# Two banks for the buckets' sums, one-hots for two buckets at once, and four smaller edits in a graph kernel

## The chip, the cores and the metric

The kernel runs on one core of one Trainium2 chip. A core has five engines with instruction queues of their own: TensorE (PE for matmuls, PEld for the loads of its stationary operand), VectorE (DVE), ScalarE (ACT), GpSimd (POOL) and SyncE (SP, which issues most of the plain DMAs). They meet by semaphores. The metric is the device time of one execution in microseconds, the median of several runs.

## The reference

A message-passing step of an equivariant graph network, all in float32: N = 10,000 nodes with 64 channels of 4 components, E = 640,000 edges with random ends `src` and `dst`.

```
R   = silu(edge_feat @ w_rad)                   # (E, 64), edge_feat is (E, 4)
xs  = x[src]                                    # (E, 64, 4)
tp  = einsum('eci,ef,ifo->eco', xs, Y, cg)      # (E, 64, 4), Y is (E, 4), cg is (4, 4, 4)
msg = R[:, :, None] * tp
agg = segment_sum(msg, dst, N)                  # (N, 64, 4)
out = einsum('ncm,cd->ndm', agg, w_mix)         # (N, 64, 4)
```

## The kernel before, in words

The nodes are cut into 313 **buckets** of at most 32 nodes, and the buckets into 20 **groups** of 15 or 16. The edges, 5000 tiles of 128, are cut into three parts by `SPLIT` (1488, 1776 and 1736 tiles). Each part is sorted by destination in two passes, and then its messages are computed bucket by bucket. Five tiles of 128 slots hold a bucket's edges of the first part, six those of the second and of the third.

**Sorting.** A pass takes chunks of T tiles (`pass1` sorts edges into groups with T = 16 in the first part and T = 24 in the others, 74 and 73 chunks; `pass2` sorts a group's edges into buckets with T = 24). `digits` and `tables` count the edges of each (tile, digit) and turn the counts into a table of starting places for several chunks at once: a count by matmul (`cnt`), a scan on VectorE (`sums`), small matmuls (`prep`, `fo`), and arithmetic on [chunks, digits]. The table that the chunks use, `sb`, holds places times the number of digits B plus the digit, as two bf16 rows. `route` then moves the chunks, in half-chunks called pieces: `places` spreads the table over the partitions by matmuls into PSUM (`pp`), `placed` copies it out on ScalarE (`pc`), `slots` finds each edge's row and slot on VectorE, `spread` builds the products `X` of slot masks and payloads on VectorE (in the first part, the last `self.spare` tiles of each piece on GpSimd), `onehots` builds a one-hot matrix per tile (the last `self.act` tiles on ScalarE), `move` runs one float32 matmul per tile with the one-hots as stationary operand, `evict` copies the result out on ScalarE, and `store` scatters its rows to DRAM with an indirect DMA of GpSimd. An edge's payload is 9 words: a key of source and destination, Y and edge_feat. `chunk` in `pass1` puts it together in `Wt`.

**Messages.** `messages` goes over units; a unit is one bucket in one part, so there are 3 × 313 = 939. For unit k: `index` (per group) takes source rows and local node numbers from the payload; `gather` issues one indirect DMA per tile on GpSimd for the rows of x, into one of seven buffers `xg`; `rests`, `spell`, `turn`, `turned`, `radial` and `silu` compute R with bf16 pieces of edge_feat through TensorE and ScalarE; `spots` compares local node numbers with 0 to 31 into `eq` and multiplies by Y, which gives `S`; `products` multiplies the gathered rows by R in place; `sums` runs two float32 matmuls per tile and adds up `G`, 128 × 256 numbers, in PSUM; `evict` takes `G` out: a copy on ScalarE in the first part (`Gp`), an addition to the earlier parts' sums `old` on VectorE in the second (`Gp`) and third (`Gs`). `fetch` loads `old` from DRAM on SP's queue, and the sums of the first two parts are stored by SP too. In the third part `full` and `mix` end four buckets with 8 float32 matmuls and write the output.

**Order of the work.** The sort of the first part runs alone in the first 750 us or so, with a compiler's order on all engines but SP. After that the order on TensorE, VectorE and ScalarE is the one in which the code emits the instructions. `groups` interleaves three streams: `messages`, `pass2` one group ahead, and `pass1` of the next part. `messages` emits a step in four quarters, given by `quarters` (line 1048): each entry is a function and how many units ahead of k it works. After each quarter the two sorts emit some of theirs. Unit k's sums come in the first quarter of step k, its eviction in the third, behind the products of unit k+1.

**PSUM.** Eight banks: one for constants and masks (`dv`, of which columns 128 to 511 are `vmsk`, the place of `eq` and of the slot masks), one `misc` for `cnt`, `prep`, `fo` and the mix, one `pos` for `pp`, two `route`, two `pre` and one `G`. `self.held` is a lock on `misc` in the order of emission, and `self.pos` one on `pos`: a stream that finds them taken yields "held", and `groups` lets the holder go on.

```
            if k % 2 and 0 <= k + 7 < NP:
                while self.pos:
                    yield "held"
                self.pos = ps.key
                places((k + 7) // 2)
            if k % 2 == 0 and 0 <= k + 6 < NP:
                placed((k + 6) // 2)
                self.pos = None
```

## Time and profile before

| | us |
|---|---|
| median of 3 runs | 9961.38 |
| lowest, highest | 9958.73, 9973.47 |
| the profiled execution | 9973.83 |
| its span, first to last instruction | 9971.9 |
| mean granted TensorE clock | 0.824 |

| engine | busy us | share of the span |
|---|---|---|
| PE | 7409.9 | 74% |
| PEld | 6726.3 | 67% |
| DVE | 6683.2 | 67% |
| ACT | 4025.3 | 40% |
| POOL | 5821.9 | 58% |

The profile names an instruction by its line in the kernel, its engine, and the tiles that it writes and reads (`G<-S,xg` is written to G and reads S and xg). "Idle before" is the time in which the engine stood just before an instruction, and the name behind `<-` is what ended most of it. "issue" means that nothing the profile shows was waited for, and "remote" that a semaphore ended the wait whose setter the profile could not name. A float32 matmul is recorded as two matmul instructions and two loads. The granted clock is the share of its full rate that TensorE was given.

### The profile page before, as it was taken

Reading aid. Unit: us, or ns where it says so; the run is one execution under the profiler, and the core shown is the slowest. Engines: PE = TensorE matmul, PEld = TensorE weight load, DVE = VectorE, ACT = ScalarE, POOL = GpSimd, SP = SyncE. Lnnn points to the kernel's source line nnn. Section 1 sums busy time; section 2 is a strip of 40 time slices with the busy share of each in tenths; the row PEclk is TensorE's granted clock in tenths of the full one; section 3 lists DMA queues with packets and bytes.
Section 4 is the critical chain, followed back from the end, with each engine's and each line's share of the span. In section 5 each row is a group of like instructions: output and inputs, shape, how many; then the busy total and the mean of one; then the engine's idle time right before and its main releaser. Section 6 shows DMA issues by size and latency. Waiting matters only on the chain. (4 is left out here: it accounts for less than half of the span.)

```text
span 9971.9 us, 143192 instructions
## 1 busy us (share of the span) xinstructions
PE 7409.9 (74%) x50081; PEld 6726.3 (67%) x50081; DVE 6683.2 (67%) x11771; ACT 4025.3 (40%) x11208; POOL 5821.9 (58%) x6222
## 2 busy tenths in 40 slices
PE   6886777877787678877777777676677776777764
PEld 5765776777776677776667677665666666676664
DVE  7885677777776677777777777565555555565543
ACT  4663454555554444444334344232232332332220
POOL 3635555555556556655555656666666666666663
PEclk8987888888887888888888888877888887888886
DMA  5113333333333334443433444444333333333331
GB/s 233 47 37 101 105 101 100 106 103 103 104 106 106 108 108 119 121 118 112 119 107 109 119 117 114 126 120 119 110 108 112 113 109 109 113 111 110 111 110 55
DMA packets 680544, 1086.82 MB, mean 109 GB/s; under 512 B 255649, under 2 KB 485103, under 8 KB 673552
## 3 DMA queue, kind: packets, MB, share of 16 engines
q0 software_dynamic: 282224, 774.67, 26.9%
q1 hardware_dynamic: 396448, 295.26, 10.1%
q8 instruction: 397, 6.50, 0.3%
q10 hardware_dynamic: 1152, 7.74, 0.2%
q14 instruction: 323, 2.65, 0.1%
HBM read 855.30 MB, written 222.79 MB: 108 GB/s over the span
## 5 line engine op out<-in xcount | busy, mean ns | idle before, releaser
L894 POOL DMA_INDIRECT xg<-in_x_dram,sidx x5321 | 5086.7, 956 | 3282.7 <-issue 1401.3
L982 PE MATMUL G<-S,xg 128*128 128x128 f32 x21284 | 3263.0, 316 | 951.4 <-issue 405.5
L982 PEld LDWEIGHTS G<-S,xg 128*128 128x128 f32 x21284 | 3049.4, 228 | 1054.0 <-issue 477.5
L612 PE MATMUL pr<-X,oh 128*128 128x81 f32 (+14 forms) x20530 | 3034.9, 306 | 731.5 <-issue 377.9
L612 PEld LDWEIGHTS pr<-X,oh 128*128 128x128 f32 x20530 | 2849.3, 215 | 859.5 <-issue 476.0
L971 DVE TENSOR_TENSOR xg<-xg,pre 128x1536 f32<-128x1536 f32 (+1 forms) x939 | 1557.6, 1659 | 413.7 <-ACT pre L953 294.3
L601 ACT ACTIVATE oh<-i,row 128x128 f32<-128x128 f32 x5322 | 1654.3, 391 | 94.9 <-PE pr L612 83.9
L585 DVE TENSOR_TENSOR X<-dv,Wt 128x2052 f32<-128x2052 f32 (+11 forms) x814 | 1336.9, 1642 | 414.8 <-remote 176.7
L953 ACT ACTIVATE pre<-pre 128x384 f32<-128x384 f32 (+1 forms) x939 | 430.8, 459 | 2491.6 <-remote 938.3
L964 DVE TENSOR_TENSOR S<-dv,pay 128x768 f32<-128x768 f32 (+1 forms) x939 | 857.6, 913 | 220.6 <-remote 111.8
L602 ACT ACTIVATE oh<-oh,ones 128x768 f32<-128x768 f32 (+1 forms) x1000 | 862.6, 863 | 31.4
L1011 DVE TENSOR_TENSOR Gs<-old,G 128x256 f32<-128x256 f32 x313 | 131.7, 421 | 1053.8 <-remote 603.6
L597 DVE TENSOR_TENSOR oh<-dv,row 128x768 f32<-128x768 f32 (+3 forms) x960 | 796.9, 834 | 6.8 <-PE pr L612 6.7
L941 ACT ACTIVATE sT<-pre 108x256 bf16<-108x256 bf16 x939 | 354.0, 377 | 703.8 <-remote 389.0
L552 ACT ACTIVATE pc<-pp 128x480 f32<-128x480 f32 (+8 forms) x500 | 236.1, 472 | 799.2 <-remote 260.5
L937 PE MATMUL pre<-idb,E 128*108 128x128 bf16 x1878 | 295.1, 241 | 313.0 <-DVE xg L971 124.8
L937 PEld LDWEIGHTS <-E 128*108 128x108 bf16 x1878 | 226.3, 143 | 381.8 <-issue 185.9
L631 POOL DMA_INDIRECT grp<-rt,idx x240 | 274.6, 1144 | 300.4 <-DVE dv L579 60.0
L949 PE MATMUL pre<-wr,sT 108*128 108x192 bf16 x1878 | 331.9, 260 | 136.0 <-ACT sT L941 76.0
L631 POOL DMA_INDIRECT bkt<-rt,idx x260 | 260.3, 1001 | 280.2 <-ACT rt L624 88.1
L1011 DVE TENSOR_TENSOR Gp<-old,G 128x256 f32<-128x256 f32 x313 | 130.8, 418 | 435.0 <-remote 257.5
L1030 PE MATMUL po<-wf,Gs 128*128 128x256 f32 (+1 forms) x1280 | 323.4, 408 | 33.0 <-DVE kov L524 17.6
(277 smaller groups left out, 5062.3 us busy)
## 6 DMA issues: line engine op xcount, KB each, us to landing
xg<-in_x_dram,sidx POOLq DMA_INDIRECT x5321
sums<-Gp SPq DMA_DIRECT2D x626, 128.0 KB
old<-sums SPq DMA_DIRECT2D x626, 128.0 KB
bkt<-z SPq DMA_DIRECT2D x26, 1024.0 KB
grp<-z SPq DMA_DIRECT2D x16, 1024.0 KB
pay<-bkt SPq DMA_DIRECT2D x208, 54.0 KB
out_dram<-ot SPq DMA_DIRECT2D x69, 128.0 KB
grp<-z ACTq DMA_DIRECT2D x7, 1024.0 KB
```

Source lines behind the costliest of these rows:

```text
L585: eng.tensor_tensor(X[:, b:e], msk[:, b:e].unsqueeze(3).to_broadcast([P, e - b, w, W]), CH[c][1][:, a + b:a + e, :].unsqueeze(2).to_broadc ...
L597: nc.vector.tensor_tensor(oh[:, :v, :], self.v128.unsqueeze(1).to_broadcast([P, v, P]), row[:, a:a + v].unsqueeze(2).to_broadcast([P, v, P ...
L601: nc.scalar.activation(oh[:, u], self.i128[:, :oh.shape[2]], AF.Square, bias=row[:, a + u:a + u + 1], scale=-1.0)
L602: nc.scalar.activation(oh[:, v:m], oh[:, v:m], AF.Relu, bias=self.ones[:, 0:1], scale=-2.0)
L612: nc.tensor.matmul(PR[c][:, ps.lo[t] * W:ps.hi[t] * W], oh[:, u, :], Xs[u], start=(t == 0), stop=(t == sizes[c] - 1), skip_group_check=True)
L631: nc.gpsimd.indirect_dma_start(out=ps.dst, out_offset=bass.IndirectOffsetOnAxis(ap=idx[:Q, i:i + 1], axis=0), in_=RT.pop(c), in_offset=None)
L894: nc.gpsimd.indirect_dma_start(out=xg[:, t, :], out_offset=None, in_=self.x, in_offset=bass.IndirectOffsetOnAxis(ap=si[:, u:u + 1], axis=0))
L937: nc.tensor.transpose(to[:108, h * P:(h + 1) * P], E[:, o + h * 108:o + h * 108 + 108], self.idb)
L953: nc.scalar.activation(RT[k], RT[k], AF.Silu)
L964: nc.vector.tensor_tensor(S[:, :ut], self.eq[:, :ut].unsqueeze(3).to_broadcast([P, ut, NB, 4]), pb[:, :, 1:5].unsqueeze(2).to_broadcast([P ...
L971: nc.vector.tensor_tensor(V, V, R.unsqueeze(3).to_broadcast([P, ut, 64, 4]), op=OP.mult)
L982: nc.tensor.matmul(G[:, h].rearrange("p n f -> p (n f)"), V[:, t, 32 * h:32 * h + 32, :].rearrange("p c i -> p (c i)"), S[:, t].rearrange( ...
```

## The change

It has six parts.

1. `G` gets two PSUM banks instead of one. The bank comes from `pos`: `pp` now lives in `misc`. In the messages the eviction comes one unit later (`evict` at -1), `full` at -2, `fetch` at 2 in the last quarter instead of 4 in the first, and `old` has three buffers instead of four.
2. In `route`, `places` and `placed` are emitted together at the end of each odd step, when `misc` is free, and `self.pos` is gone.
3. `spots` works on every second unit and makes `eq` and `S` for two buckets at once; `S` and `eq` are twice as long, and `dlc` is laid out so that two buckets' numbers lie side by side.
4. In `tables`, the counts are multiplied by B as ScalarE copies them from PSUM, and the lower bounds `low` carry the factor and the digit from the start, so `sums` holds places as the table wants them. `at` and its scaling go; the bf16 copy is made on ScalarE; the row of totals is divided by B again on VectorE. The two copies `ovr` and, in `pass1`, the copy of the key into `Wt` move from VectorE to ScalarE.
5. First-pass chunks of the second and third part have 22 tiles instead of 24 (81 and 79 chunks).
6. One-hot matrices have Q columns instead of 128 (Q is 120 in the first pass, 128 in the second), and `self.spare` in the first part is 4 instead of 3.

```diff
-        early, late = some(16), some(T)
+        early, late = some(16), some(22)
...
-        self.eq = self.vmsk[:, :UT * NB].rearrange("p (t n) -> p t n", n=NB)
+        self.eq = self.vmsk[:, :2 * UT * NB].rearrange("p (t n) -> p t n", n=NB)
...
-        nc.scalar.activation(cols[:, :, 1:m + 1], cnt[:H, :m * B].rearrange("p (t b) -> p b t", b=B), AF.Copy)
+        nc.scalar.activation(cols[:, :, 1:m + 1], cnt[:H, :m * B].rearrange("p (t b) -> p b t", b=B), AF.Copy,
+                             scale=float(B))
...
-        n = w("n", B, 32)
-        nc.vector.tensor_copy(n[:N], sums[:N, :, m])
+        n, ni = w("n", B, 32), w("ni", B, 32, d=I32)
+        nc.vector.tensor_scalar(ni[:N], sums[:N, :, m], 1.0 / B, 0.5 / B - 0.5, op0=OP.mult, op1=OP.add)
+        nc.vector.tensor_copy(n[:N], ni[:N])
+        sb = wk.tile([H, ps.T * B], BF, name="sb", tag="sb" + ps.key, bufs=3)
+        tb = sb[:, :m * B].rearrange("p (t b) -> p b t", b=B)
+        nc.scalar.activation(tb, sums[:, :, :m], AF.Copy)
...
-        nc.vector.scalar_tensor_tensor(tb(at), sums[:, :, :m], float(B),
-                                       self.v128[:H, :B].unsqueeze(2).to_broadcast([H, B, m]), op0=OP.mult, op1=OP.add)
-        nc.vector.tensor_copy(sb[:, :m * B], at[:, :m * B])
-        nc.vector.tensor_tensor(sb[32:, :m * B], at[32:, :m * B], sb[32:, :m * B], op=OP.subtract)
+        nc.vector.tensor_tensor(tb[32:], sums[32:, :, :m], tb[32:], op=OP.subtract)
...
-        nc.vector.tensor_copy(two[:, 0], rep(over[:N, :B]))
-        nc.vector.tensor_copy(two[:, 1], rep(inc[:N]))
+        nc.scalar.activation(two[:, 0], rep(over[:N, :B]), AF.Copy)
+        nc.scalar.activation(two[:, 1], rep(inc[:N]), AF.Copy)
...
-            pp = self.ps.tile([P, 512], F, name="pp", tag="pos", bufs=1)[:, :m * B]
+            pp = self.ps.tile([P, 512], F, name="pp", tag="misc", bufs=1)[:, :m * B]
...
-            oh = self.ph.tile([P, ps.H, P], F, name="oh", bufs=3)
+            oh = self.ph.tile([P, ps.H, P], F, name="oh", bufs=3)[:, :, :Q]
...
-            if k % 2 and 0 <= k + 7 < NP:
-
-                while self.pos:
-                    yield "held"
-                self.pos = ps.key
-                places((k + 7) // 2)
-            if k % 2 == 0 and 0 <= k + 6 < NP:
-                placed((k + 6) // 2)
-                self.pos = None
...
+            if k % 2 and 0 <= k + 7 < NP:
+                while self.held:
+                    yield "held"
+                places((k + 7) // 2)
+                placed((k + 7) // 2)
...
-            nc.vector.tensor_copy(Wt[:, :m, 0].bitcast(I32), SB[b][:, o:o + m])
+            nc.scalar.activation(Wt[:, :m, 0], SB[b][:, o:o + m].bitcast(F), AF.Copy)
...
+            if j % 2:
+                return
+            ut = tiles(k)[1]
+            b = min(2, self.nb(g[1]) - j)
+            n = b * ut
+            pb = self.pay[g][:, j:j + b].rearrange("p b (t w) -> p (b t) w", w=W)
+            dl = IDX[g][1][:, j * ut:(j + b) * ut]
+            nc.vector.tensor_tensor(self.eq[:, :n], self.i32.unsqueeze(1).to_broadcast([P, n, NB]),
+                                    dl.unsqueeze(2).to_broadcast([P, n, NB]), op=OP.is_equal)
+            S = ph.tile([P, 2 * UT, NB, 4], F, name="S")
+            nc.vector.tensor_tensor(S[:, :n], self.eq[:, :n].unsqueeze(3).to_broadcast([P, n, NB, 4]),
+                                    pb[:, :, 1:5].unsqueeze(2).to_broadcast([P, n, NB, 4]), op=OP.mult)
+            for i in range(b):
+                SS[k + i] = S[:, i * ut:(i + 1) * ut]
...
-                GP[g, j] = self.ps.tile([P, 2, NB, 4], F, name="G", tag="G", bufs=1)
+                GP[g, j] = self.ps.tile([P, 2, NB, 4], F, name="G", tag="G", bufs=2)
...
-                OLD[g, j] = ph.tile([P, 2, 4, NB], F, name="old", bufs=4)
+                OLD[g, j] = ph.tile([P, 2, 4, NB], F, name="old", bufs=3)
...
-        quarters = (((index, LI), (gather, LG), (fetch, 4), (turn, 2), (sums, 0), (silu, 1)), ((rests, 4), (turned, 2), (spots, 1)),
-                    ((products, 1), (evict, 0)), ((spell, 3), (radial, 2), (full, -1)))
+        quarters = (((index, LI), (gather, LG), (turn, 2), (sums, 0), (silu, 1)), ((rests, 4), (turned, 2), (spots, 1)),
+                    ((products, 1), (evict, -1)), ((spell, 3), (radial, 2), (full, -2), (fetch, 2)))
...
-            self.rt_bufs, self.ls, self.act, self.spare = 20, 10, 3, 3
+            self.rt_bufs, self.ls, self.act, self.spare = 20, 10, 3, 4
```

41 lines of the change are left out of this document (17 added, 24 removed).

## The prediction

> **What bounds the kernel now.** I read the page's busy shares first, then the busy time by stage. The second part of the run (from 830 us) has three stages, one for each share of the edges; they end where the `Gp` evictions move from ScalarE to VectorE and become `Gs`. Columns: us, busy time and instructions of PE, PEld, DVE, ACT and POOL, granted clock, DMA share, GB/s.
>
> ```profile
> span 9971.9 us, 143192 instructions
> ...
> PE 7409.9 (74%) x50081; PEld 6726.3 (67%) x50081; DVE 6683.2 (67%) x11771; ACT 4025.3 (40%) x11208; POOL 5821.9 (58%) x6222
> ...
> 0.00:830.00 830.00, 628.93 (x4242) 541.67 (x4242) 650.52 (x1566) 486.39 (x1433) 354.11 (x525) 0.85 0.30 102
> 830.00:3680.00 2850.00, 2202.32 (x15297) 2013.05 (x15297) 2040.32 (x3598) 1388.88 (x3923) 1665.11 (x1727) 0.84 0.37 105
> 3680.00:6917.00 3237.00, 2440.97 (x16619) 2223.71 (x16617) 2303.13 (x3691) 1279.70 (x3458) 1938.93 (x2021) 0.83 0.41 117
> 6917.00:9854.00 2937.00, 2107.18 (x13836) 1928.45 (x13837) 1651.55 (x2746) 865.16 (x2375) 1846.79 (x1934) 0.81 0.38 110
> ```
>
> No engine is full in any stage. With 313 buckets a stage, a bucket takes 9.1, 10.3 and 9.4 us, and PE works 7.0, 7.8 and 6.7 us of it. So waits set the pace. The list of waits (total us, times, longest) says which:
>
> ```profile
> POOL xg L894 <- issue: 1401.3, 4501, 10.2
> ACT pre L953 <- remote: 938.3, 149, 20.0
> ...
> POOL xg L894 <- PE G L982: 782.3, 220, 14.1
> DVE Gs L1011 <- remote: 603.6, 114, 10.9
> ...
> PE G L982 <- DVE Gs L1011: 279.7, 67, 11.0
> ACT pc L552 <- remote: 260.5, 34, 14.2
> ...
> ACT pc L552 <- PE pp L546: 201.7, 54, 10.7
> ...
> PE G L982 <- DVE Gp L1011: 171.6, 42, 9.2
> ...
> PE pre L937 <- DVE xg L971: 124.8, 86, 6.1
> ...
> PE pr L612 <- DVE oh L597: 104.9, 51, 8.5
> ...
> PE G L982 <- ACT Gp L1013: 81.0, 29, 8.7
> ```
>
> The largest wait of PE for anyone is for the eviction of the one bank `G`: 279.7 + 171.6 + 81.0 = 532 us in 138 waits. The evictions themselves wait for PE, often under the name "remote". POOL too waits for PE's sums to free a gather buffer, so it too could go faster than it is let. A stretch of the timeline (start, length, engine) shows the knot:
>
> ```profile
> 9563.54 2.94 PE L982 MATMUL G<-S,xg 128*128 128x128 f32 x24 [1.27 <-DVE Gs L1011]
> ...
> 9566.49 0.28 PE L937 MATMUL pre<-idb,E 128*108 128x128 bf16 x2
> ...
> 9573.92 0.95 POOL L894 DMA_INDIRECT xg<-in_x_dram,sidx  x1 [0.31 <-issue]
> 9577.32 0.42 DVE L1011 TENSOR_TENSOR Gs<-old,G 128x256 f32<-128x256 f32 x1 [10.91 <-remote]
> 9577.42 0.47 ACT L953 ACTIVATE pre<-pre 128x384 f32<-128x384 f32 x1 [12.52 <-remote]
> 9577.56 0.95 POOL L894 DMA_INDIRECT xg<-in_x_dram,sidx  x1 [2.69 <-remote]
> ...
> 9577.80 4.42 PE L982 MATMUL G<-S,xg 128*128 128x128 f32 x19 [11.04 <-DVE Gs L1011]
> ```
>
> PE's sums are over by 9566.5 on record, yet the eviction, the silu and POOL's next gather all start within 0.24 us at 9577.3, 2.4 us after POOL's last gather ended (9573.92 + 0.95). I read that as PE's completions reaching the others late while POOL streams gathers. Whatever the reason, PE and DVE both stand for 11 us here, because the next sums need the bank, the bank needs the eviction, and the eviction needs the late completion.
>
> **The change part by part.** The sum starts from the profiled execution, 9973.8 us (span 9971.9 and 1.9 around it); that is 12.4 above the median of the runs, 9961.4.
>
> (A) *Second bank for `G`, eviction one bucket later.* In such a stall PE may now run the next bucket's sums: their products were finished before it (the eviction follows them on DVE). Then it stops at the radial matmuls, whose input ACT copies only after a completion of PE. So a stall gives back at most one bundle of sums, 2.94 us by the row above: 138 × 2.94 = 406 us; many of the 138 are shorter (mean 3.9 us). I take −300, between 0 (the same late completion holds the silu, and nothing comes sooner) and −532. DVE and, in the first stage, ACT no longer hold the work queued behind the eviction (spread and one-hots of the sort), which is why I stay near the upper half. `fetch` moves three buckets ahead of its use instead of four, 3 × 9.4 = 28 us before the eviction, and passes the sort's loads on SP's queue; 128 KB would take 1.2 us at the 110 GB/s of the third stage's row, an estimate, so 0, and if it were late the eviction would hold DVE again. `full` one later: one step at the very end, 0.
>
> (B) *Less on DVE.* The forms that carry it (busy, mean ns):
>
> ```profile
> L964 DVE TENSOR_TENSOR S<-dv,pay 128x768 f32<-128x768 f32 x626 | 599.5, 958 | 26.5 <-remote 5.0
> ...
> L964 DVE TENSOR_TENSOR S<-dv,pay 128x640 f32<-128x640 f32 x313 | 258.2, 825 | 194.1 <-remote 106.8 <-PE G L982 29.2 <-PE pre L937 23.6
> ...
> L961 DVE TENSOR_TENSOR dv<-dv,dlc 128x192 f32<-128x192 f32 x626 | 226.0, 361 | 6.8
> ...
> L734 DVE COPY Wt<-si 128x24 int32<-128x24 int32 (+2 forms) x240 | 50.6, 214 | 51.3 <-POOL X L585 51.3
> ...
> L484 DVE SCALAR_TENSOR_TENSOR at<-sums,dv 64x336 f32<-64x336 f32 (+7 forms) x92 | 76.5, 832 | 0.0
> ...
> L486 DVE CAST sb<-at 64x336 bf16<-64x336 f32 (+7 forms) x92 | 33.4, 363 | 3.0
> ...
> L500 DVE COPY ovr<-inc 4x128 f32<-4x128 f32 (+4 forms) x92 | 22.3, 242 | 0.1
> ...
> L585 DVE TENSOR_TENSOR X<-dv,Wt 128x2052 f32<-128x2052 f32 x131 | 300.7, 2296 | 48.5 <-PE pr L612 28.1 <-remote 8.9 <-issue 4.6
> ...
> L585 DVE TENSOR_TENSOR X<-msk,Wt 128x540 f32<-128x540 f32 (+1 forms) x186 | 184.4, 994 | 25.9 <-ACT Wt L733 25.9
> ```
>
> 128 more elements cost `S` 133 ns, so 1.04 ns each, and 160 ns are fixed; `dv`, by the same slope, has about 160 fixed too. One pair saves one of each, 0.33 us; 13 groups of 16 buckets and 7 of 15 make 153 pairs a stage, 459 in all: −150. `at` goes (−76), its cast moves to ACT (−33); a conversion of a row's last column is added (+15). Two `ovr` copies like the one shown and the `Wt` copy move to ACT (−42, −51). Chunks of 22 tiles are at most 18 slots wide where 24 tiles reached 19: from the slot bounds in the code the products shrink by 31,400 elements (−33), and one-hots of 120 columns give about −20; 13 more chunks and 2 more tables bring +40. In all about −350 of 6683. Little of it is on the path: apart from the eviction, PE waits for DVE for 125 + 105 us, 3% of the time. I take −40, between 0 and −350. The pair's longer `S` (958 → 1757 ns) delays the products every second bucket by 1.1 us; the second bank covers that.
>
> (C) *ACT, and places and placed together.* ACT gets the copies, about +150 us of 4025; its idle time before the silu, 938 us under "remote" alone, hides them. The new wait is the other one: `placed` now stands directly behind its matmuls, where it stood half a step later, so ACT must wait for PE's 0.8 us and a completion that may be late; queued behind it on ACT are silu, turned and one-hots, and PE waits for those. It also shares `misc` with tables and mix. Before, 88 such waits cost ACT 462 us. The stages have 160 + 260 = 420 chunks. From 0 (ACT would have stood anyway) to 420 × 1.4 = 590 us; I take +60, near the end at which ACT has slack.
>
> (D) *13 more chunks* (81 + 79 for 74 + 73), each with a store on POOL (row below) and about 2 us on ACT and 0.8 on PE: 17 us on POOL, 26 on ACT; +20 (0 to 40).
>
> (E) *First stage (to 830 us, DVE 78% busy).* One of five product tiles goes to POOL: a fifth of 184.4 us, −37 on DVE, with its share of (B); POOL, at 43%, takes about a third more of its products and stays below. −25, between 0 and −60.
>
> (F) *One-hots of 120 columns as PE's stationary operand, narrower moving one.* No first-pass row shows 120 columns. The nearest is the final mix, 128 against 96:
>
> ```profile
> L631 POOL DMA_INDIRECT grp<-rt,idx x240 | 274.6, 1144 | 300.4 <-DVE dv L579 60.0 <-ACT rt L622 57.4 <-DMA grp<-z 49.2
> ...
> L612 PEld LDWEIGHTS pr<-X,oh 128*128 128x128 f32 x20530 | 2849.3, 215 | 859.5 <-issue 476.0 <-ACT rt L622 130.0 <-DVE oh L597 113.9
> ...
> L1030 PEld LDWEIGHTS po<-wf,Gs 128*128 128x128 f32 x1168 | 227.8, 200 | 57.2 <-issue 15.4 <-DVE kov L524 8.0 <-DVE ko L522 2.4
> ...
> L1030 PEld LDWEIGHTS po<-wf,Gs 128*96 128x96 f32 x112 | 24.8, 229 | 22.8 <-DVE kov L524 11.9 <-issue 0.7
> ```
>
> By these rows fewer columns load no faster (229 against 200 ns): 10,000 first-pass loads × 29 ns = +290 at worst; the narrower chunks' moving operand saves some 40. A gain for columns in proportion would be 200 × 8/128 = 12 ns, −125. I take −30. The Trainium skill (TensorE: Matmul & The Clock Gate, LDWEIGHTS) says that a load takes its columns ÷ 1.2 in ns; by that, eight columns are 6.7 ns, an estimate of −67 us, which would make the sum 9562 in place of 9599; the row of 96 columns does not agree, though the clock may differ between the two rows.
>
> (G) *Clock.* Two stretches, before and after the stall shown above, granted clock after the busy times:
>
> ```profile
> 9554.00:9567.00 13.00, 10.44 (x94) 9.91 (x91) 6.63 (x8) 3.47 (x10) 8.95 (x10) 1.00 0.43 127
> 9578.00:9583.00 5.00, 5.00 (x24) 5.00 (x25) 3.10 (x4) 0.18 (x1) 3.78 (x5) 0.50 0.38 108
> ```
>
> PE idles and comes back at half rate (24 sums in 2.94 us before, 19 in 4.42 after). With fewer stalls I put the stages' clock 0.011 up: 7409.9 × 0.011/0.83 = 98 us less PE work, two thirds on the path, −60 (0 to −200, at 0.85). The Trainium skill's same page (A second HAM failure mode: psum-queue depth-cycling) speaks against the change: a kernel that went round its PSUM banks paused so often between groups of matmuls that its clock swung between half and full. By that rule (G) is 0 and the sum 9659; the trace has the swing already with one bank, in the two rows above.
>
> Sum: −300 −40 +60 +20 −25 −30 −60 = −375; 9973.8 − 375 = 9599, and 12 less against the median: **9590 us**, −3.7%.
>
> **Rivals.**
> 1. *The wait moves to the silu.* In the stall shown, ACT's silu stood 12.5 us for the same moment. If every stall is like that, (A) keeps 60 and (G) nothing: 9973.8 − 60 − 15 = 9899, 9890 against the median. For: ACT's 938 us for "remote". Against: PE's own listed wait is for the bank, not for the silu.
> 2. *Slower: ACT stands at `placed`.* Its price in (C) grows from +60 to +590, on top of the other terms (−435 without C): 10,129 − 12, about 10,115. It decides from 435/420 = 1.04 us a chunk that reach PE. For: the 88 waits average 5.3 us. Against: ACT is busy 29 to 49% in the stages.
> 3. *The knot opens altogether and POOL paces.* Then a stage lasts as long as its gathers: 0.95 + 0.30 us each, as the timeline's spacing shows; 6 a bucket are 7.5 us, 5 are 6.25, and stores on top make 7.0, 8.2 and 7.9 a bucket. 313 × 23.1 = 7230; half of the 1794 us between that and the three stages' 9024 would give about 9065, a third 9365. I name 9200.
> 4. *Narrow one-hots load slower*, (F) at +290: 9973.8 − 375 + 320 − 12 = 9907.
>
> **How the numbers follow.** Forecast 0.53 (9300 to 9800), rival 1 0.14, rival 2 0.14, rival 3 0.14, rival 4 0.05. Runs of before lie within 0.15% of each other, so 0.2% is about what can be told from no change. Faster: 0.53 + 0.14 + 0.05 + 0.11 of rival 1 = 0.83; same 0.04 (rival 1 with (C) a little dearer, or a mild rival 2); slower 0.13. The range goes from 9200 to 9980: it leaves out nearly all of rival 2 and the better half of rival 3, 2 in 10.
>
> **What would show it.** (A) right: PE's wait for `Gp`/`Gs` near zero, DVE's idle before it gone; wrong: the same microseconds at PE before the radial matmuls or the sums, released by ACT or products. (B): `S` as 128x1536, 470 times or so. (C): `pc` idle over 462 us, with PE or silu waiting behind it. (F): mean of the first-pass weight load above or below 215 ns. (G): stage clock above 0.84. POOL's wait for `G` should shrink by some 300 us. The prediction is wrong if PE's completions stay as late, since POOL would then stream longer between pauses and hold everything else back.

## The result, and the profile after

The kernel after took 10,082.8 us (median of four runs) against 9,960.1 for the kernel before: 1.0116 times its time, 95% interval 1.0099 to 1.0134. Predicted were 9,590. In three later comparisons of the same two kernels the ratio was 1.0077 [1.0051, 1.0103], 1.0095 [1.0064, 1.0127] and 1.0084 [1.0056, 1.0113]; the change costs about 1%.

The head of the page after, and its busy time by stage (columns as in the prediction):

```profile
span 10063.5 us, 141956 instructions
...
PE 7460.0 (74%) x50156; PEld 6755.0 (67%) x50156; DVE 6528.4 (65%) x10500; ACT 4277.0 (42%) x11973; POOL 5872.2 (58%) x6231
```

```profile
0.00:884.00 884.00, 653.90 (x4344) 561.56 (x4344) 696.86 (x1462) 517.90 (x1623) 387.00 (x528) 0.82 0.28 97
884.00:3771.00 2887.00, 2212.32 (x15306) 2028.40 (x15306) 1971.41 (x3208) 1482.92 (x4219) 1679.08 (x1737) 0.82 0.36 104
3771.00:7035.00 3264.00, 2425.37 (x16649) 2218.54 (x16649) 2230.87 (x3300) 1372.60 (x3696) 1957.21 (x2031) 0.81 0.40 116
7035.00:9944.00 2909.00, 2138.35 (x13772) 1927.26 (x13771) 1591.67 (x2362) 898.42 (x2416) 1831.97 (x1920) 0.82 0.38 110
```

Against before, the time ahead of the first eviction grew from 830 to 884 us, the next two stages by 37 and 27, and the last shrank by 28. Of the 54 us ahead of the first eviction, 8 come from the eviction's own place, one bucket later than before; the first sums start at 825 us before and at 871 after. So half of the loss lies ahead of the first bucket's sums, where one would not look for the cost of a bank for `G`.

From the list of waits of the kernel after (total us, times, longest), and the groups of instructions that answer to the prediction's signs:

```profile
DVE xg L976 <- ACT pre L953: 1237.9, 284, 16.6
...
POOL xg L894 <- PE G L987: 809.0, 215, 11.8
ACT pc L555 <- remote: 798.5, 117, 15.7
ACT pre L953 <- remote: 625.1, 113, 15.5
...
ACT pc L555 <- PE pp L549: 458.4, 152, 9.2
...
PE pre L949 <- ACT sT L941: 297.1, 94, 13.3
```

```profile
L976 DVE TENSOR_TENSOR xg<-xg,pre 128x1536 f32<-128x1536 f32 (+1 forms) x939 | 1560.3, 1662 | 1786.5 <-ACT pre L953 1237.9 <-issue 266.0 <-DMA xg<-in_x_dram,sidx 207.1
...
L967 DVE TENSOR_TENSOR S<-dv,pay 128x1536 f32<-128x1536 f32 (+1 forms) x480 | 785.1, 1636 | 50.7 <-remote 28.8 <-PE G L987 5.0
...
L555 ACT ACTIVATE pc<-pp 128x440 f32<-128x440 f32 (+9 forms) x513 | 242.6, 473 | 1619.5 <-remote 798.5 <-PE pp L549 458.4 <-DVE pos L564 88.4
...
L482 ACT ACTIVATE sb<-sums 64x440 bf16<-64x440 f32 (+7 forms) x94 | 170.8, 1833 | 113.4 <-DVE sums L475 63.9 <-issue 46.4 <-DVE Gp L1016 2.1
L490 DVE TENSOR_TENSOR sb<-sums,sb 32x440 bf16<-32x440 f32 (+7 forms) x94 | 166.4, 1770 | 55.4 <-ACT sb L482 43.0 <-issue 9.3 <-ACT Wt L733 1.3
...
L1016 DVE TENSOR_TENSOR Gs<-old,G 128x256 f32<-128x256 f32 x313 | 129.7, 414 | 5.5 <-PE G L987 5.5
```

The wait at the eviction is gone: 5.5 us before `Gs`. In its place VectorE stands at the products, for ACT's silu (1,238 us), and ACT stands 1,620 us before it copies `pp`. PE's wait for `sT` ahead of the radial matmuls grew from 76 to 297 us, and POOL's wait for `G`, which should have shrunk by some 300 us, grew from 782 to 809. The prediction's knot is still there, one instruction further on:

```profile
9802.74 0.46 PE L949 MATMUL pre<-wr,sT 108*128 108x192 bf16 x2 [2.23 <-issue]
...
9803.86 0.41 DVE L1016 TENSOR_TENSOR Gs<-old,G 128x256 f32<-128x256 f32 x1
...
9804.33 1.65 PE L987 MATMUL G<-S,xg 128*128 128x128 f32 x6
...
9808.20 0.94 POOL L894 DMA_INDIRECT xg<-in_x_dram,sidx  x1 [0.30 <-issue]
...
9811.70 0.47 ACT L953 ACTIVATE pre<-pre 128x384 f32<-128x384 f32 x1 [9.01 <-remote]
9811.84 0.94 POOL L894 DMA_INDIRECT xg<-in_x_dram,sidx  x1 [2.70 <-remote]
...
9812.21 1.75 DVE L976 TENSOR_TENSOR xg<-xg,pre 128x1536 f32<-128x1536 f32 x1 [7.93 <-ACT pre L953]
```

The eviction runs with no wait, and PE does go on to the next sums. But the radial matmuls, over at 9803.2 on record, reach ACT only at 9811.7: 2.6 us after POOL's last gather ended. Then silu, products and gather all start within 0.5 us.

### The profile page after: what moved, and what is told of

It is laid out like the page before. It is cut to its first block, busy times and chain, and to the rows that moved or that the text cites. A ratio compares the mean times of both kernels' runs of the same rounds, so it can differ in the third digit from the quotient of the medians.

```text
span 10063.5 us, 141956 instructions
## 1 busy us (share of the span) xinstructions
PE 7460.0 (74%) x50156; PEld 6755.0 (67%) x50156; DVE 6528.4 (65%) x10500; ACT 4277.0 (42%) x11973; POOL 5872.2 (58%) x6231
## 5 line engine op out<-in xcount | busy, mean ns | idle before, releaser
L615 PE MATMUL pr<-X,oh 128*120 128x162 f32 (+18 forms) x20530 | 3009.5, 306 | 712.1 <-issue 321.1
L615 PEld LDWEIGHTS pr<-X,oh 128*120 128x120 f32 (+1 forms) x20530 | 2827.1, 215 | 826.7 <-issue 416.4
L604 ACT ACTIVATE oh<-i,row 128x120 f32<-128x120 f32 (+1 forms) x5478 | 1687.9, 389 | 116.2 <-PE pr L615 59.5
L588 DVE TENSOR_TENSOR X<-dv,Wt 128x1287 f32<-128x1287 f32 (+9 forms) x840 | 1308.5, 1558 | 644.6 <-PE pr L615 239.6
L555 ACT ACTIVATE pc<-pp 128x440 f32<-128x440 f32 (+9 forms) x513 | 242.6, 473 | 1619.5 <-remote 798.5
L605 ACT ACTIVATE oh<-oh,ones 128x768 f32<-128x768 f32 (+3 forms) x1026 | 869.3, 847 | 28.5
L967 DVE TENSOR_TENSOR S<-dv,pay 128x1536 f32<-128x1536 f32 (+1 forms) x480 | 785.1, 1636 | 50.7 <-remote 28.8
L600 DVE TENSOR_TENSOR oh<-dv,row 128x600 f32<-128x600 f32 (+4 forms) x986 | 759.6, 774 | 4.7 <-PE pr L615 4.5
L949 PEld LDWEIGHTS <-sT 108*128 108x128 bf16 x1878 | 180.4, 109 | 540.0 <-ACT sT L941 326.5
L548 PE MATMUL pp<-sb,id 64*128 64x440 bf16 (+9 forms) x513 | 181.9, 355 | 303.2 <-ACT pc L555 81.4
```

The lines of the kernel that those rows point to most:

```text
L588: eng.tensor_tensor(X[:, b:e], msk[:, b:e].unsqueeze(3).to_broadcast([P, e - b, w, W]), CH[c][1][:, a + b:a + e, :].unsqueeze(2).to_broadc ...
L600: nc.vector.tensor_tensor(oh[:, :v], self.v128[:, :Q].unsqueeze(1).to_broadcast([P, v, Q]), row[:, a:a + v].unsqueeze(2).to_broadcast([P, ...
L604: nc.scalar.activation(oh[:, u], self.i128[:, :oh.shape[2]], AF.Square, bias=row[:, a + u:a + u + 1], scale=-1.0)
L605: nc.scalar.activation(oh[:, v:m], oh[:, v:m], AF.Relu, bias=self.ones[:, 0:1], scale=-2.0)
L615: nc.tensor.matmul(PR[c][:Q, ps.lo[t] * W:ps.hi[t] * W], oh[:, u, :], Xs[u], start=(t == 0), stop=(t == sizes[c] - 1), skip_group_check=True)
L949: nc.tensor.matmul(R[:, h * 192:h * 192 + n * 64], sT[:n * 36, h * P:(h + 1) * P], self.wr[:n * 36, :n * 64], start=True, stop=True)
```

## The experiments

Three theories stood at the start. Theory 1: the second bank gives back much of its 300 us, and `pp` in `misc`, with ACT standing at `placed`, takes that and 100 us more. Theory 2: the bank gives little, since the same late completions hold the silu. Theory 3: the other parts cost.

The runs stand in five groups; those of a group ran on one chip beside the kernel before, and each ratio is of one group (`e6` to `e8` are one execution each). In two of the groups the same kernel before took 8,307 us, not 9,960 to 10,000; its time stands with each heading. What differs are PE's completions, as the second group shows. A completion is the semaphore update by which the others learn that PE's matmuls are done. The expectations of the first group are written for a kernel before of 9,960 us; I read them as shares of that.

### First group (before: 8,307.8 us): which part

`e1_banks`, the kernel before with these edits (shortened; `full` comes one unit later too):

```diff
-pp = self.ps.tile([P, 512], F, name="pp", tag="pos", bufs=1)
+pp = self.ps.tile([P, 512], F, name="pp", tag="misc", bufs=1)
+places((k + 7) // 2); placed((k + 7) // 2)
-G ... bufs=1   (evict, 0)   old bufs=4 (fetch, 4)
+G ... bufs=2   (evict, -1)  old bufs=3 (fetch, 2) in the last quarter
```

> The kernel before with parts 1 and 2 of the change alone: two G banks, evict one bucket later, three old buffers with fetch in the last quarter, pp in misc and places and placed together. Whole result computed. Theory 1 (the second G bank gives back a good part of its 300 us, and pp in misc, with ACT standing at placed, takes that and 100 us more): 10,020 to 10,150 us, ACT's idle before pc over 1,300 us (after: 1,619.5), VectorE's wait at evict near zero. Theory 2 (the G bank gives nothing, because the same late sums come back as a wait at the silu; placed costs little): 9,930 to 10,000. Theory 3 (the loss comes from the other parts: spare 4, paired S, ACT's copies): 9,650 to 9,850.

Measured 8,385.1 us, 1.0088 [1.0071, 1.0105]: 77 us slower, in theory 1's range alone (1.006 to 1.019).

`e2_rest`, the kernel after with those edits undone:

> The kernel after without parts 1 and 2: one G bank, evict in its own bucket, four old buffers, pp in its own bank with placed half a step behind places; all the other parts stay. Whole result computed. Theory 1: 9,840 to 9,960 (the kernel before less what paired S saves on VectorE, plus some 50 us in the first fill), with ACT's idle before pc back near 800 us. Theory 2: the same as theory 1 here, 9,900 to 10,000. Theory 3: 10,040 to 10,120, as slow as the kernel after.

Measured 8,334.1 us, 1.0029 [1.0017, 1.0042], a little above theory 1's range (0.988 to 1.000) and inside theory 2's (0.994 to 1.004). The groups of the page for the copy of `pp`, and the first and last start of the first stage's evictions, first of `e1_banks` (two fences), then of `e2_rest`:

```profile
L552 ACT ACTIVATE pc<-pp 128x480 f32<-128x480 f32 (+8 forms) x500 | 237.0, 474 | 1442.7 <-PE pp L546 928.2 <-DVE pos L561 416.8 <-DVE ci L567 29.6
```

```profile
L1009 ACT ACTIVATE Gp<-G x313: 356/377/409, 846.7 to 3183.2; 128x256 f32<-128x256 f32 x157
```

```profile
L555 ACT ACTIVATE pc<-pp 128x440 f32<-128x440 f32 (+8 forms) x513 | 239.3, 466 | 518.9 <-DVE pos L564 314.6 <-PE pp L549 189.2 <-PE pre L953 3.8
```

```profile
L1022 ACT ACTIVATE Gp<-G x313: 356/383/702, 809.2 to 3129.3; 128x256 f32<-128x256 f32 x157
```

With `pp` shared, ACT's wait for its matmuls grows from 189 to 928 us, and the first eviction comes 38 us later, of which 7 are its own place one bucket later. So most of the loss sits in the banks' part; that it sits there in `pp`, not in `G`, the next run supports. Theory 3 has 26 us, theory 1 is supported.

`e3_split`, the kernel after with (shortened; the lock on `misc` is told of the new holder in three more places)

```diff
-places((k + 7) // 2)
-placed((k + 7) // 2)
+places((k + 7) // 2); self.held = ps.key + "p"     # odd k
+placed((k + 6) // 2); self.held = None             # even k, half a step later
```

> The kernel after, with placed half a step behind places again, and misc held from one to the other, so that ACT reaches pc when pp is long done; the price is that other users of misc wait for it. Whole result computed. Theory 1: ACT's idle before pc falls from 1,619.5 us to under 1,000, and the time by 60 to 250 us, to 9,830 to 10,020. Theory 2: within 40 us of the kernel after (10,040 to 10,110), because ACT's idle moves from pc to the silu. Theory 3: as theory 2.

Measured 8,330.4 us, 1.0024 [1.0014, 1.0033]. Against `e2_rest`, the second bank, `pp` in `misc` and holding `misc` half a step longer cost nothing that shows. What is left of part 2 as the cost is that `places` and `placed` come together, at the end of the step: `placed` then stands directly behind `pp`'s matmuls, and `places` comes later in the step. These two were not run apart.

`e4_own`, the kernel after with a bank of its own for `pp`, split as before the change, and two buffers for `old`; VectorE's constants and masks give up their bank and lie in SBUF:

```diff
-self.dv = self.ps.tile([P, 512], F, name="dv", tag="dv", bufs=1)
+self.dv = c.tile([P, 384], F, name="dv")
```

> The kernel after with a bank of its own for pp and placed half a step behind places, as before the change, and the two G banks kept; VectorE's constants and masks give up their bank and lie in SBUF, and old has two buffers, fetched one bucket ahead. Whole result computed. Theory 1: the gain of the second bank without its price: 9,650 to 9,850. Theory 2: within 50 us of the second run of this call (one G bank, own bank for pp). Theory 3: 10,020 to 10,120. Masks in SBUF can shift all of these by some tens of us, since VectorE's one-hot rows then read and write SBUF alone.

Measured 9,348.1 us, 1.1248 [1.123, 1.1267], which no theory had. POOL's gathers, in `e2_rest` and then here:

```profile
L898 POOL DMA_INDIRECT xg<-in_x_dram,sidx x5321 | 5109.0, 960 | 1784.7 <-issue 1451.6
```

```profile
L897 POOL DMA_INDIRECT xg<-in_x_dram,sidx x5321 | 6171.1, 1160 | 1640.6 <-issue 1467.1
```

Each gather takes 200 ns longer once VectorE's constants and masks lie in SBUF, 1,062 us in all, about the whole loss, since POOL has almost no idle time but its issue gaps there. So this run tells nothing of `pp`.

### Second group (before: 9,999.7 us): without the gathers

Theory 4 came from the first group's traces, in which TensorE's completions arrive at once: there POOL's gathers pace, and the change can only add to the time ahead of the first gather.

> The kernel after, unchanged, beside the kernel before. In the first comparison the two took 10,082.8 and 9,960.1 us; in the call of the four earlier experiments the same kernel before took 8,307.8 us. Theory 4 (where TensorE's completions arrive at once, as in the traces of those four, POOL's gathers pace the span, and the change can only add to the time ahead of the first gather): 1.002 to 1.010 of the kernel before if it takes about 8,308, POOL's idle before the gathers outside the fill under 400 us. Theory 1 (pp in misc costs ACT wherever it runs): over 1.010, with ACT's idle before pc well above the kernel before's. If the kernel before takes about 9,960 again: 1.010 to 1.013 by both.

`e5_after`: 10,071.7 us, 1.0077 [1.0051, 1.0103], in the condition of the first comparison and a little below the 1.010 to 1.013 expected there.

> The kernel before, unchanged, for a trace beside the other one of this call. Theory 4, if it takes about 8,308: its wait for the one G bank (1,489 us of VectorE's idle before the evict in the first trace) is below 300 us, since nearly all of TensorE's completions are then prompt, and POOL's gathers run on without a pause in over 90% of their span; the second bank then has nothing left to give. Theory 2 of the earlier call would show the same wait as in the first trace.

`e6_before`: 9,984.5 us, so the other condition of theory 4 did not come; it is the mark for the next two, in which the only edit is (shortened)

```diff
-for t in range(ut): nc.gpsimd.indirect_dma_start(out=xg[:, t, :], in_=self.x, in_offset=...)
+nc.sync.dma_start(xg[:, :ut], self.x[r0:r0 + P * ut].rearrange("(p t) c -> p t c", t=ut))
```

> The kernel after with the gathers of x left out: each bucket's tiles are filled by one plain read of a fixed block of x, issued on SP's queue; so the sums are of wrong rows, and POOL has no gathers to issue. Theory 4: TensorE's completions are prompt all through, the time falls below 8,000 us, and VectorE (6,528 us busy) or TensorE (7,460 us busy by the first trace) paces it. If the completions are late for another reason than POOL's gathers, the time stays near that of the kernel after.

> The kernel before with the same gathers left out in the same way. It tells what the change is worth where POOL neither paces nor delays. My prediction's step A (the second bank gives 300 us) would show as 200 to 350 us between this kernel and the one before it in this call; theory 1 (the bank's gain is eaten at pp) as less than 50 us either way.

`e7_plain_after`: 7,523.3 us; `e8_plain_before`: 7,465.3 us. VectorE's evictions in `e6_before`, and in `e8_plain_before`:

```profile
L1011 DVE TENSOR_TENSOR Gs<-old,G 128x256 f32<-128x256 f32 x313 | 131.6, 420 | 1042.6 <-remote 555.7 <-PE G L982 255.5 <-PE pre L937 124.7
L1011 DVE TENSOR_TENSOR Gp<-old,G 128x256 f32<-128x256 f32 x313 | 130.7, 418 | 429.8 <-remote 252.4 <-PE G L982 87.5 <-PE pre L937 46.6
```

```profile
L1008 DVE TENSOR_TENSOR Gs<-old,G 128x256 f32<-128x256 f32 x313 | 130.5, 417 | 188.7 <-PE G L979 185.9 <-DMA xg<-in_x_dram 0.3
L1008 DVE TENSOR_TENSOR Gp<-old,G 128x256 f32<-128x256 f32 x313 | 129.9, 415 | 39.3 <-PE G L979 35.0 <-issue 2.3
```

VectorE's 1,472 us before the evictions are 228 without gathers, with the one bank still in place. The wait was not for a bank, it was for late completions. And with PE and VectorE the busiest (86 to 89%) the change still costs 58 us, of which 47 lie ahead of the first sums (798 us before, 845 after): step A's 200 to 350 are not there, and theory 1's "less than 50 either way" is only nearly met.

How late PE's completions are can be worked out from the trace: for each matmul that updates a semaphore, the time from its recorded end (which is modelled) to the next update on record, from 900 us on to 200 us ahead of the end.

```
kernel            updates  within 0.1 us  over 1 us  mean
before              3593        34%          47%     2.16 us
after               3831        36%          47%     2.12 us
f3_banks2           3620        34%          49%     2.20 us   (third group)
e8_plain_before     3530       100%           0%     0.02 us   no gathers
e1_banks            3739       100%           0%     0.02 us   before at 8,308
h2_t22              3608       100%           0%     0.02 us   before at 8,307
```

About a tenth of the updates have no record where they are late (3,662 for 4,052 in the kernel before). Taken the other way, from each recorded update back to the last end before it, the mean in the kernel before is 1.7 us, and 42% are over 1 us; so the size is rough, the difference is not. In the kernels before and after, about 99% of the updates of the first 600 us, ahead of any gather, are prompt. So the gathers delay PE's completions, by about 2 us in the mean, but only where the kernel before takes 9,960 to 10,000. Whether it is POOL's issuing or the traffic of single rows, no run tells: the edit takes away both. In the other condition the same gathers run and nothing is late. There a bucket goes like this (`h2_t22`, POOL gathering all along):

```profile
8006.16 0.94 POOL L892 DMA_INDIRECT xg<-in_x_dram,sidx  x1 [0.30 <-issue]
...
8006.69 0.33 PE L947 MATMUL pre<-wr,sT 108*128 108x192 bf16 x2
...
8007.10 0.47 ACT L951 ACTIVATE pre<-pre 128x384 f32<-128x384 f32 x1 [2.02 <-issue]
8007.40 0.95 POOL L892 DMA_INDIRECT xg<-in_x_dram,sidx  x1 [0.30 <-issue]
```

The silu starts 0.1 us after the matmuls' end, against 8.5 us in the stretch of the kernel after.

### Third group (before: 9,974.2 us): what the bank alone is worth

Theory 5 was formed here: `pp`'s sharing costs about 50 us in the first fill and more behind it, the other parts some 25.

> The kernel after, unchanged, as the mark for the other three of this call. So far it took 1.0116 and 1.0077 times the kernel before where that took 9,960 to 10,000 us (TensorE's completions late while POOL issues gathers), and 58 us more than it with the gathers left out. Theory 5 (pp in misc, issued together with placed, costs about 50 us in the first fill and more behind it, in either condition of the completions; the other parts cost some 25): where the kernel before takes 8,308, 1.009 to 1.014; else 1.007 to 1.012.

> The kernel after without the second G bank and with pp's own bank (the second experiment, 1.0029 with the kernel before at 8,308). If the kernel before takes 9,960 to 10,000 here: theory 5 says 0.997 to 1.004, since what it adds (13 chunks, ACT's copies, the larger spare) and what it saves (VectorE's paired S) are small; if the second bank were the cause of the whole loss and more, it would be below 0.995. If it takes 8,308: 1.002 to 1.004 again.

`f3_banks2` is `e1_banks` with the edit of `e3_split`: the second bank without its price.

```diff
-places((k + 7) // 2); placed((k + 7) // 2)
+places((k + 7) // 2); self.held = ps.key + "p"     # odd k
+placed((k + 6) // 2); self.held = None             # even k
```

> The kernel before with the second G bank, evict one bucket later, and pp in misc, but placed half a step behind places as before, misc being held from one to the other; none of the other parts. My prediction's step A: 0.96 to 0.975 of the kernel before where that takes 9,960 (its 1,489 us of waits for G's sums then give back their 300 us). Theory 2 (the same late completions come back as waits at the silu, so the bank itself is worth little): 0.993 to 1.003. Where the kernel before takes 8,308, both say 0.998 to 1.003, since POOL then paces.

`f4_split_spare3` is `e3_split` with

```diff
-self.rt_bufs, self.ls, self.act, self.spare = 20, 10, 3, 4
+self.rt_bufs, self.ls, self.act, self.spare = 20, 10, 3, 3
```

> The kernel after with placed half a step behind places and misc held between (the third experiment, 1.0024 with the kernel before at 8,308), and besides with the spare of the first pass at 3, as before the change. If the larger spare costs, by the VectorE products that got longer though they got smaller (1,367 ns for 128x576 against 1,158 for 128x720): 15 to 30 us below the third experiment, so 0.999 to 1.001 where the kernel before takes 8,308. If it doesn't matter: 1.002 to 1.003. Where the kernel before takes 9,960: 0.99 to 1.004 by theory 5, 0.96 to 0.975 by my step A.

Measured: `f1_after` 10,074.0 us, 1.0095 [1.0064, 1.0127]; `f2_rest` 9,987.9, 1.0016 [1.0002, 1.0030]; `f3_banks2` 9,914.6, 0.9938 [0.9918, 0.9958]; `f4_split_spare3` 9,966.3, 0.9991 [0.9976, 1.0005].

The bank is worth 62 us of 9,974, a fifth of step A, and `f3_banks2` beats both kernels. What became of the rest is in its list of waits:

```profile
ACT pre L951 <- remote: 990.6, 160, 15.3
DVE S L962 <- remote: 906.6, 185, 10.9
POOL xg L892 <- PE G L980: 762.2, 224, 11.8
...
DVE xg L969 <- ACT pre L951: 451.7, 153, 12.2
```

VectorE, let past the eviction, stops at the next `S` and at the products. Its idle time before the evictions fell from 1,489 us to 5, but before `S` it grew from 221 to 1,266, and before the products from 414 to 667: of 2,123 us in all, 1,937 are left. I read the wait at `S` as one for a buffer that PE has read and not yet reported. This is theory 2 for the bank.

`f2_rest`, the other parts with one bank, costs 16 us, inside the range of theory 5.

The evictions of the first two stages, in `f1_after` and in `f4_split_spare3`:

```profile
L1018 ACT ACTIVATE Gp<-G x313: 356/377/702, 890.1 to 3773.1; 128x256 f32<-128x256 f32 x157
L1016 DVE TENSOR_TENSOR Gp<-old,G x313: 402/414/418, 3786.4 to 7042.0; 128x256 f32<-128x256 f32 x157
```

```profile
L1020 ACT ACTIVATE Gp<-G x313: 352/377/697, 811.0 to 3693.6; 128x256 f32<-128x256 f32 x157
L1018 DVE TENSOR_TENSOR Gp<-old,G x313: 402/414/418, 3702.8 to 6941.2; 128x256 f32<-128x256 f32 x157
```

Splitting `places` from `placed` again, and spare 3, take 104 us off by the ratios of one group (1.0095 against 0.9991); 79 of them lie ahead of the first eviction. There no group's work runs beside the sort. I read it so that nothing covers a chunk placed late. The shared bank alone does not make it late: `f3_banks2` shares it too, and its first sums start at 824 us, those of the kernel before at 825. Whether ACT's standing does, or `places` coming later in the step, no run tells. Behind the first eviction the split is worth only some 25 us, though ACT's idle time before `pc` falls by 966, first in `f1_after`, then in `f4_split_spare3`:

```profile
L555 ACT ACTIVATE pc<-pp 128x440 f32<-128x440 f32 (+9 forms) x513 | 242.9, 473 | 1631.7 <-remote 738.2 <-PE pp L549 485.1 <-DVE pos L564 91.8
```

```profile
L555 ACT ACTIVATE pc<-pp 128x440 f32<-128x440 f32 (+8 forms) x513 | 239.9, 468 | 665.9 <-remote 376.6 <-PE pp L549 135.2 <-DVE pos L564 39.0
```

Most of it comes back as idle time before the silu, 2,086 us in the first and 2,709 in the second.

### Fourth group (before: 8,306.8 us): the rest of the parts

> The kernel after with placed half a step behind places again and misc held between, the spare left at 4: the same kernel as the third experiment, meant to stand where the kernel before takes 9,960 to 10,000. Theory 5: pp's sharing alone costs 70 to 110 us there (57 in the first fill, by the start of the first group's sums at 890 us against 833 to 811 in the traces without it), so 0.999 to 1.003, and the spare of 4 accounts for about 20 us between this kernel and the last one of the earlier call. If pp's sharing were only the fill: 1.003 to 1.006. Where the kernel before takes 8,308: 1.002 to 1.003 again.

`h1_split` is `e3_split` again: 8,332.8 us, 1.0029 [1.0018, 1.0040].

`h2_t22` is `f3_banks2` with

```diff
-early, late = some(16), some(T)
+early, late = some(16), some(22)
```

> The kernel before with the second G bank and the split pp (0.9938 in the earlier call), and chunks of 22 tiles in the first pass; nothing else. If the 13 more chunks are what costs the other parts their 50 us: 0.997 to 1.002. If they cost what my step D said (20 us) and start the second pass some 20 us earlier: 0.993 to 0.996.

8,293.0 us, 0.9985 [0.9976, 0.9995], the fastest kernel of this condition. The number lies in the range for dear chunks, but that range was meant for late completions; where POOL paces it tells only that bank and chunks together do not cost.

`h3_single` is `f4_split_spare3` with `S` made for one bucket at a time:

```diff
-S = ph.tile([P, 2 * UT, NB, 4], F, name="S")
+S = SS[k] = ph.tile([P, UT, NB, 4], F, name="S")
```

> The last kernel of the earlier call (after, split pp, spare 3: 0.9991) without the paired one-hots: S is made for one bucket at a time, as before the change. If pairing saves VectorE's 70 us of busy time usefully, this is slower than that: 1.001 to 1.005. If pairing costs, because one pair's S holds its place until both buckets' sums are known to be done, this is faster: 0.993 to 0.996.

8,354.5 us, 1.0052 [1.0035, 1.0069]: 22 us slower than `h1_split` although its spare is the smaller. Pairing `S` helps, here by some 20 us, and by more if the smaller spare helps.

`h4_dve` is `f4_split_spare3` with

```diff
-nc.scalar.activation(Wt[:, :m, 0], SB[b][:, o:o + m].bitcast(F), AF.Copy)
+nc.vector.tensor_copy(Wt[:, :m, 0].bitcast(I32), SB[b][:, o:o + m])
-nc.scalar.activation(two[:, 0], rep(over[:N, :B]), AF.Copy)   (and two[:, 1])
+nc.vector.tensor_copy(two[:, 0], rep(over[:N, :B]))           (and two[:, 1])
-nc.scalar.activation(tb, sums[:, :, :m], AF.Copy)
+nc.vector.tensor_copy(tb, sums[:, :, :m])
```

> The last kernel of the earlier call (0.9991) with the three copies that the change gave to ACT (the table's upper part, over and inc, the tag column) on VectorE again. If ACT's extra work, in front of sT and silu, is what costs: 0.993 to 0.996. If not, VectorE's busy time goes up by some 100 us and the time by 0 to 30 us: 0.999 to 1.003.

8,305.6 us, 0.9998 [0.9988, 1.0007], the number expected if ACT's extra work costs nothing; that was reckoned from a run with late completions. Against `h1_split` it is 27 us less, of which the spare has some, and no slower for VectorE's longer work.

The spare shows in the first eviction of `h1_split` (spare 4), then of `h3_single` (spare 3), which differ ahead of it in little else:

```profile
L1020 ACT ACTIVATE Gp<-G x313: 352/377/702, 807.4 to 3140.2; 128x256 f32<-128x256 f32 x157
```

```profile
L1014 ACT ACTIVATE Gp<-G x313: 352/377/702, 788.2 to 3134.4; 128x256 f32<-128x256 f32 x157
```

The larger spare costs 19 us there.

### Fifth group (before: 9,981.4 us): ACT's copies where completions are late

> The kernel of the run before in the last call (after, split pp, spare 3, the three copies on VectorE: 0.9998 with the kernel before at 8,307), meant to stand where the kernel before takes 9,960 to 10,000. There the same kernel with the copies on ACT took 0.9991, and the second bank with split pp alone 0.9938. If ACT's copies are what costs there too: 0.992 to 0.996. If not: 0.998 to 1.002. Where the kernel before takes 8,307: 0.999 to 1.001 again.

`i1_dve` (the kernel of `h4_dve`): 9,942.2 us, 0.9958 [0.9945, 0.9971], against 0.9991 [0.9976, 1.0005] with the copies on ACT in the third group. They cost some 33 us, a difference of two groups. Ahead of the first eviction they save instead: it comes at 811 us with the copies on ACT and at 832 with them on VectorE, so behind it they cost more than the 33.

> The kernel after, unchanged, meant to stand where the kernel before takes 8,307. The sum of the parts there: pp's sharing with the second bank 77 us, the other parts 26 us, so 1.009 to 1.014, with most of the loss ahead of the first bucket's sums (about 850 to 870 us against 806). Where the kernel before takes 9,960 to 10,000: 1.007 to 1.012 again.

`i2_after`: 10,072.6 us, 1.0084 [1.0056, 1.0113]. It did not meet the condition that it was meant for; the whole change was not measured where completions are prompt.

## Why the prediction was wrong

The sum, in the condition of the prediction, from the ratios and some 9,975 us: second bank −62 (`f3_banks2`); paired `S`, chunks of 22, 120 columns and scaled tables together +20 (`i1_dve` less `f3_banks2`); ACT's copies +33 (`f4_split_spare3` less `i1_dve`); `placed` behind `places`, with spare 4, +104 (`f1_after` less `f4_split_spare3`), of which the spare is about 19. That makes +95, as it must, since the terms are a chain of differences that ends at `f1_after` (0.95%); the two differences between groups (+20 and +33) are the less certain ones, and the +20 lies within the intervals. The terms also depend on the order in which the parts are added. With the other parts in place, one bank took 1.0016 (`f2_rest`, spare 4), two banks and the split 0.9991 (`f4_split_spare3`, spare 3): 25 us, of which the spare is about 19. So the bank's 62 us are its worth on top of the kernel before; beside the other parts next to nothing of them shows.

(A) is the step that failed, and decided the direction: −300 was taken between bounds of 0 and −532, −62 measured. The stalls and the 2.94 us a stall stand in the rows; what failed is the choice between the ends. The prediction had itself the row for the lower one, the silu 12.5 us late for the same moment, and kept it as rival 1, in which "(A) keeps 60". That rival's mechanism is what the traces show, and the prediction's own sign of it came, with PE standing ahead of the radial matmuls. PE's own list of waits names the bank because, as I read the stretch, the eviction was only the first of several instructions that needed the same completion.

(C) is the term that was mis-sized: +60 taken, about +118 measured. Of these about 85 are `placed` behind `places` (104 less the spare's 19). The other 33 are ACT's copies, which (C) put at nothing because idle time before the silu would hide them; ACT's work grew by 252 us, not 150. Rival 2 named ACT's standing at `placed`, and its sign, `pc`'s idle time over 462 us, came at 1,257 (798.5 + 458.4). But the prediction looked for its price in the stages, and there it is small: most of the 85 lies in the first fill, which no term covered. Rival 2 came nearest in time (10,115), but by other terms: it kept A's 300.

(B) VectorE fell by 155 us, not 350. Pairing was right: `S` and `eq` fell by 146 us together, 150 predicted. The table was not, and is 114 of the 195 us missing. Before, its three steps took 161 us: 76.5 and 33.4 by the prediction's rows, and

```profile
L487 DVE TENSOR_TENSOR sb<-at,sb 32x336 bf16<-32x336 f32 (+7 forms) x92 | 51.1, 555 | 3.1
```

Of these only `at` was written through the transposed view. After, the bf16 copy writes through it and the subtraction reads and writes through it, and they take 1,833 and 1,770 ns (rows of the kernel after above): 3.6 us a table, not 1.75, and half of it on ACT, ahead of silu and `sT`. The prediction counted 33 us for the moved cast and nothing for the subtraction. (PE's waits for VectorE, 125 + 105 us, are 2.3% of the time, not 3%.)

(D) was not taken apart. (E) had the wrong sign: −25 taken, +19 measured where completions are prompt. (F): the mean load stayed at 215 ns in the first comparison, and rival 4 did not come. That mean goes over both passes, and only the first has 120 columns. By form, in `h4_dve`:

```profile
L615 PEld LDWEIGHTS pr<-X,oh 128*128 128x128 f32 x10530 | 1309.5, 202 | 188.2 <-ACT rt L625 59.0 <-DVE oh L600 57.0 <-ACT oh L605 33.6
```

```profile
L615 PEld LDWEIGHTS pr<-X,oh 128*120 128x120 f32 x10000 | 1234.9, 195 | 203.1 <-DVE oh L600 82.0 <-ACT rt L625 30.8 <-issue 25.4
```

In the kernel after it is 220 and 209 ns. Here width and pass change together. Between 60 and 580 us only the first pass runs: there five kernels with 128 columns took 204 to 209 ns a load in the mean, six with 120 columns 196 to 202. So eight columns less save about 7 ns, near the 6.7 that the Trainium skill's rule (TensorE: Matmul & The Clock Gate, LDWEIGHTS) gives, an estimate. The prediction's row of 96 columns, 229 ns, had pointed the wrong way. Of the 67 us that these 6.7 ns would be, no run shows how much reaches the time.

(G) The stages' clock was 0.82, 0.81 and 0.82, not 0.011 higher than 0.84, 0.83 and 0.81. The second bank is not what lowered it; `f3_banks2` has it too, and what did, no run tells:

```profile
830.00:3636.00 2806.00, 2188.64 (x15286) 1995.70 (x15286) 2034.94 (x3589) 1374.59 (x3912) 1666.05 (x1729) 0.84 0.38 107
3636.00:6881.00 3245.00, 2462.99 (x16625) 2231.43 (x16625) 2297.09 (x3717) 1279.44 (x3460) 1947.06 (x2026) 0.82 0.41 117
6881.00:9790.00 2909.00, 2127.02 (x13743) 1907.37 (x13743) 1624.64 (x2720) 862.59 (x2364) 1835.71 (x1924) 0.81 0.39 110
```

The last sentence of the prediction, that it is wrong if PE's completions stay as late, is what happened: 2.16 us late in the mean before, 2.12 after.

## What to carry to other kernels

When several engines wake within half a microsecond of each other, the wait that the list names is only the last of a set: a buffer that releases one of them is worth what the next one leaves over, here a fifth at best. Before a bank is given to one user, price the user that has to share instead, and in the first fill too, where no other work runs beside the sort. Price a step that is merged with a transposition by a row with that transposition, not by its contiguous predecessor.

## What the runs showed of the hardware that was not expected

The same program ran in 8,307 us in two groups and in 9,960 to 10,000 in the others, and the whole of it goes with PE's completions: prompt in the one, 2 us late in the mean in the other, and there only while POOL issues gathers. What sets the condition stays open; the programs were the same, and the third and the fourth group, which carry the same chip number, show one condition each. Where they are prompt, POOL paces: in `e2_rest` its gathers work 5,109 us and idle 1,785, of which 1,452 are the gaps between two issues. Rival 3's 7,230 us for the stages is near what `h1_split` leaves behind its first eviction, 8,333 − 807.

Constants and masks of VectorE in SBUF rather than PSUM took each of POOL's gathers from 960 to 1,160 ns (`e4_own`). And the spare of 4 made VectorE's products longer though smaller; the forms before and after:

```profile
L585 DVE TENSOR_TENSOR X<-msk,Wt 128x720 f32<-128x720 f32 x93 | 107.7, 1158 | 0.0
```

```profile
L588 DVE TENSOR_TENSOR X<-msk,Wt 128x576 f32<-128x576 f32 x93 | 127.1, 1367 | 1.7 <-PE pr L615 1.7
```

In both, VectorE has two operands in SBUF while POOL works. The Trainium skill (SBUF — State Buffer, Who interferes with whom) says that such an operation contends with GpSimd instructions that read SBUF, over a port pair that is held exclusively; the products agree, with one more of VectorE's five tiles on POOL: 1,367 ns for 576 columns, 1,158 for 720. Of GpSimd's generation of DMA descriptors the same section infers that VectorE's `tensor_tensor` does not stall it. If that is what a gather spends on POOL, the 200 ns here differ; no run takes a gather apart further.
